# TensorE's program walked through once before it is run: a loop of two rounds over four parts

## The chip, the cores and the metric

The kernel runs on one core of one Trainium2 chip. The core has five engines with a program each: TensorE (PE in the profile, its weight loads PEld), VectorE (DVE), ScalarE (ACT), GpSimd (POOL) and SyncE (SP, which here only issues DMAs), and 16 DMA engines that move data between HBM and the core's memory. The metric is the device time of one execution in microseconds (us): 344.06 for the kernel before, the median of three runs (343.95 to 344.22).

## The reference

Two branches over the same two vectors x (2 x 1 x 512), mixed by a gate. Branch A is one decode step of attention with 32 heads over a cache of 4096 keys and values of length 128 for each of two batches; branch B is a small feed-forward network.

```python
g = _sigmoid((x * gate_w).sum(-1, keepdims=True))
q = (x @ wq).reshape(B, Sq, 32, 128).transpose(0, 2, 1, 3)
scores = jnp.einsum("bhqd,bhkd->bhqk", q, k_cache) * (128 ** -0.5)
o = jnp.einsum("bhqk,bhkd->bhqd", softmax(scores), v_cache)
a = o.transpose(0, 2, 1, 3).reshape(B, Sq, 4096) @ wo
b = jnp.einsum("bsf,fd->bsd", jnp.maximum(jnp.einsum("bsd,df->bsf", x, w1), 0), w2)
return g * a + (1 - g) * b
```

The caches are 64 MB each in bfloat16 and are read once; with the weights 145.4 MB go through the core.

## The kernel before

Each engine's program is collected first, as a list of operations in the order in which the functions at the end of the kernel are called (lines 703 to 740): gate, q_proj, ffn_h and ffn_relu, 64 k_turn, k_scores, softmax, v_unit(0), v_loop, gathers, the last two v_unit, project, last_rows, store. Then `resolve` numbers the signals and `emit` (line 88) writes the list of one engine after the other, with the waits for other engines' semaphores. `seen` keeps the highest value already waited for, so that no wait is written twice.

SyncE issues all large transfers in one list (lines 325 to 342): wq, w1, ten pieces of the key cache, nine of the value cache, then w2x (24 rows of 4 KB, in two transfers), wo in two parts, and w2 in three. A piece of 8 MB fills two of five regions of the buffer `kv`, a piece of 4 MB one; each is issued when TensorE has done with what the region held. For the third key piece that is the end of turn 3 of the scores (`pe_sc_3`).

VectorE transposes each key piece in 64 turns (line 471) into the four buffers of `kt`. TensorE multiplies them with the queries in a hardware loop of 8 rounds of 8 turns (k_scores, lines 481 to 511), the values with the probabilities in a hardware loop of 3 rounds of two pieces (v_loop, lines 587 to 608). `_Loop` holds the steps of such a loop, and `emit` opens it at line 98. Everything else of TensorE's program is written out: gate (4 transposes and a sum), q_proj and ffn_h (lines 402 to 455), one value piece before v_loop and two half pieces after it (v_unit, line 570), the gathers (line 639), project (line 664) and last_rows (line 683), whose last matmuls wait for the last piece of w2. GpSimd writes masked queries for every four turns (line 395), after ScalarE's copies (line 379).

The gate waits for x and gate_w; q_proj waits for wq and for the gate's `xTw`; the first transpose of a key piece stands behind the feed-forward network's first half in VectorE's list.

## Time and profile before

| what | value |
|---|---|
| median of three runs | 344.06 us |
| profiled execution | 344.31 us |
| its span, first to last instruction | 343.0 us |
| matmuls busy | 220.4 us |
| VectorE busy | 197.2 us |
| DMA, read from HBM | 145.43 MB, 424 GB/s over the span |
| mean granted TensorE clock | 0.846 |

The page of a profile gives busy times of the engines, the span in 40 slices, the DMA queues, the chain of work that ended last, groups of instructions and DMA issues. A group line holds the source line, engine, operation, what is written from what, a count, busy time and mean, then the idle time of the engine just before such instructions and what ended it. A line of a window holds the stretch, its length, the busy time of PE, PEld, DVE, ACT and POOL with their instructions, the granted clock, the DMA share and GB/s. A line of the timeline holds the start, the time to the end, and the instructions merged in it. Queue q1 carries SyncE's transfers; the queues of the kind "instruction" carry program text.

### The profile page before, as it was taken

The page shows a single profiled execution, that of the slowest core. Times are in us where ns is not written, and L with a number is a line of the kernel's source. Part 1 is how long each engine was busy: PE and PEld are TensorE (multiplying, and loading weights), DVE is VectorE, ACT ScalarE, POOL GpSimd, SP SyncE. Part 2 cuts the span into 40 slices and gives each one's busy share as a digit, 9 for nine tenths or more (in the row PEclk, how much of TensorE's full clock was granted, in tenths as well). Part 3 has the DMA queues.
Part 4 walks back from the last instruction along what each step waited for, and adds up shares of the span by engine and source line. Part 5 has one row for each costly group of instructions (what it writes and reads, how often), then busy time and mean ns, then how long its engine had stood idle before and what let it go on. Part 6 is the DMA issues. An engine that isn't in the chain of part 4 may idle for free.

```text
span 343.0 us, 2384 instructions
## 1 busy us (share of the span) xinstructions
PE 220.4 (64%) x1236; PEld 52.7 (15%) x764; DVE 197.2 (57%) x140; ACT 10.2 (3%) x30; POOL 13.9 (4%) x38
## 2 busy tenths in 40 slices
PE   0454629889969799799799463709073542809655
PEld 0110101111111111111111121102020110202312
DVE  0247249899889899698999496230606041110621
ACT  1060000000000000000000120000000000000000
POOL 6000000000000000000000200000000000000000
PEclk9986958999989999989899966967858595876968
DMA  8998989899999999898999999898989999999995
GB/s 314 451 495 367 489 367 489 374 481 436 420 466 390 429 428 481 374 489 371 485 420 436 451 405 468 382 481 374 481 382 481 420 436 451 405 420 432 412 418 213
DMA packets 3789, 145.50 MB, mean 424 GB/s; under 512 B 427, under 2 KB 560, under 8 KB 840
## 3 DMA queue, kind: packets, MB, share of 16 engines
q1 hardware_dynamic: 3778, 145.43, 98.4%
q8 instruction: 4, 0.07, 0.1%
q14 instruction: 1, 0.01, 0.0%
q10 hardware_dynamic: 6, 0.00, 0.0%
HBM read 145.43 MB, written 0.00 MB: 424 GB/s over the span
## 4 chain that ended last, share of the span: by engine, by line
DMA 59%; DVE 19%; PE 17%; issue 4%; ACT 0%; SPq 0%; DVEq 0%
DMA kv<-in_A_v_cache_dram 25%; DMA kv<-in_A_k_cache_dram 24%; DVE kt L471 16%; PE PS L477 7%; DMA kv<-in_B_w_dram 6%; PE PS L603 4%; DMA kv<-in_A_wq_dram 4%; PE PS L498 2%; PE PS L582 2%; PE PS L400 1%; DVE qrow L424 1%; DVE mpad L514 1%; ACT kt L526 0%; PE PS L484 0%; DVE kt L530 0%
## 5 line engine op out<-in xcount | busy, mean ns | idle before, releaser
L471 DVE STREAM_TRANSPOSE kt<-kv 128x2048 f32<-128x2048 f32 x64 | 141.2, 2274 | 24.5 <-DMA kv<-in_A_k_cache_dram 24.5
L498 PE MATMUL PS<-kt,qbuf 128*128 128x512 bf16 x256 | 107.0, 418 | 32.0 <-issue 27.2
L477 PE MATMUL PS<-kt,qbuf 128*128 128x512 bf16 x256 | 106.9, 418 | 0.0
L603 PE MATMUL PS<-kv,kt 128*64 128x512 bf16 x192 | 46.5, 462 | 56.7 <-DMA kv<-in_A_v_cache_dram 56.7
L615 DVE TENSOR_TENSOR kt<-PS,maskc 32x512 f32<-32x512 f32 (+1 forms) x21 | 14.5, 689 | 89.8 <-PE PS L477 82.2
L498 PEld LDWEIGHTS PS<-kt,qbuf 128*128 128x128 bf16 x256 | 25.9, 101 | 141.5 <-issue 141.5
L477 PE MATMUL PS<-kv,kt 128*64 128x512 bf16 x192 | 45.9, 456 | 0.0
L603 PEld LDWEIGHTS PS<-kv,kt 128*64 128x64 bf16 x192 | 14.9, 132 | 96.4 <-issue 96.4
L582 PE MATMUL PS<-kv,kt 128*32 128x512 bf16 x128 | 11.5, 522 | 10.3 <-DVE kt L543 7.3
L555 DVE TENSOR_TENSOR kt<-kt,mask 128x2048 bf16<-128x2048 bf16 (+1 forms) x10 | 16.1, 1654 | 0.0
L395 POOL TENSOR_TENSOR qbuf<-qs,mask 128x64 bf16<-128x64 bf16 x16 | 6.5, 406 | 162.2 <-PE PS L477 145.6
L627 DVE TENSOR_REDUCE kt<-kt 128x128 f32<-128x512 f32 x9 | 9.2, 1019 | 0.3
L526 ACT ACTIVATE kt<-PS,negm 128x512 bf16<-128x512 f32 x4 | 2.7, 685 | 172.8 <-DVE negm L522 172.8
L400 PE MATMUL PS<-kv,xTw 128*32 128x512 bf16 (+1 forms) x32 | 5.3, 693 | 3.5 <-DMA kv<-in_A_wq_dram 3.5
L582 PEld LDWEIGHTS PS<-kv,kt 128*32 128x32 bf16 x128 | 4.7, 125 | 16.3 <-DVE kt L543 7.8
L424 DVE CAST qrow<-PS 128x256 bf16<-128x256 f32 x2 | 2.6, 1508 | 5.7 <-PE PS L477 5.7
L643 PE MATMUL PS<-kt,selx 128*32 128x128 f32 x18 | 2.9, 293 | 4.0 <-DVE kt L627 3.0
L347 PE MATMUL PS<-ident,x_sb 3*128 3x3 bf16 x4 | 0.3, 167 | 8.2 <-DMA x_sb<-in_gate_w_dram 8.2
L350 DVE COPY xT<-PS 128x12 bf16<-128x12 bf16 x1 | 0.2, 171 | 8.5 <-PE PS L347 8.5
L700 ACT ACTIVATE out_sb<-PS 2x128 bf16<-2x128 f32 x2 | 0.5, 270 | 142.3 <-PE PS L679 142.2
L514 DVE TENSOR_REDUCE mpad<-PS 128x2 f32<-128x2048 f32 x1 | 2.3, 2291 | 3.1 <-PE PS L510 3.1
L477 PE MATMUL PS<-kv,xTw 128*32 128x512 bf16 (+1 forms) x24 | 3.7, 512 | 0.0
(78 smaller groups left out, 45.2 us busy)
## 6 DMA issues: line engine op xcount, KB each, us to landing
kv<-in_A_k_cache_dram SPq DMA_DIRECT2D x4, 4096.0 KB, 29.4
kv<-in_A_v_cache_dram SPq DMA_DIRECT2D x2, 4096.0 KB, 24.4
kv<-in_A_wq_dram SPq DMA_DIRECT2D x1, 4096.0 KB, 12.5
kv<-in_A_wo_dram SPq DMA_DIRECT2D x1, 3072.0 KB, 34.2
kv<-in_B_w_dram SPq DMA_DIRECT2D x1, 1376.0 KB, 15.3
kv<-in_A_wo_dram SPq DMA_DIRECT2D x1, 1024.0 KB, 36.2
kv<-in_B_w_dram SPq DMA_DIRECT2D x1, 896.0 KB, 21.4
kv<-in_B_w_dram SPq DMA_DIRECT2D x1, 256.0 KB, 21.7
```

The costliest lines, as they stand in the source:

```text
L395: pool(lambda g: g.tensor_tensor(out=out, in0=src, in1=mask, op=ALU.mult).then_inc(sem_q[k % 2], 1), waits=waits)
L400: return e.matmul(out, lhsT=xTw[:, t, :], rhs=rhs, start=(t == 0), stop=(t == 3), tile_position=(0, 32 * c))
L424: dve(lambda v, dst=dst, src=src: v.tensor_copy(out=dst, in_=src), waits=[f"pe_qr{half}"], signal=f"qrow{half}{e2}")
L471: dve(lambda v: v.transpose(out=dst, in_=pairs[:, h, 64 * a:64 * a + 64, :]).then_inc(sem_kt[i % SPAN], 1), waits=([f"pe_sc_{i - NKT}"] if ...
L477: return e.add_instruction(mybir.InstMatmult(start_tensor_calc=start, stop_tensor_calc=stop, tile_size=size, tile_position=at, ldweights=F ...
L498: ins = e.matmul(out, lhsT=lhsT, rhs=rhs, start=False, stop=False)
L514: dve(lambda v: v.tensor_reduce(out=mpad[:, 0:2], in_=psf(0, 128, 0, 4 * BANK).rearrange("p (par n) -> p par n", par=2), axis=AX.X, op=ALU ...
L555: ins = v.tensor_tensor(out=out, in0=src.unsqueeze(2).to_broadcast(shape), in1=mask8[:].unsqueeze(1).unsqueeze(3).to_broadcast(shape), op= ...
L582: ins = e.matmul(psf(32 * t, 32 * t + 32, V_BS[n] * BANK, 512), lhsT=v_weights(n)[:, j], rhs=rows[:, :, j, :], start=(j < 4), stop=(j >= n ...
L603: ins = e.matmul(out, lhsT=lhsT, rhs=rows[:, :, k, :], start=start, stop=stop, tile_position=(0, 64 * t))
L615: dve(lambda e: e.tensor_tensor(out=parts[p0:p1], in0=psf(p0, p1, bank * BANK, 512).rearrange("p (c d) -> p c d", c=4), in1=maskc[p0:p1].u ...
L627: dve(lambda e: e.tensor_reduce(out=X2[:, b, k, :], in_=parts.rearrange("p c d -> p d c"), axis=AX.X, op=ALU.add), waits=[f"dve_m{n}"], si ...
```

## The change

Only TensorE's program is written in another way. Three calls of `part()` mark places in its list of operations: after k_scores, after the first gather (with VectorE's `pr_clear`), and after the last v_unit. That makes four parts: the front with the scores; the first value piece, v_loop and the first gather; the last two half pieces of values; the projection and the last rows. `emit_twice` opens a loop of two rounds on TensorE alone. A register `walk` is 0 in the first round and 1 in the second. At the head of each part a comparison jumps to the part if `walk` is 1 and over it if not; a part ends with a jump to the place behind it. So in the first round no operation of the kernel is carried out, and in the second all are, in the old order with the old waits. The two hardware loops now lie within the new one. The other four engines' programs stay as they were.

```diff
-    def emit(self, engine, eng):
-        seen = {}
+    def emit_twice(self, engine, eng, parts):
+        ops, seen = self.ops[engine], {}
+        walk = self.nc.alloc_registers("walk", engines=(eng.engine,))
+        self.nc.regs_mov(walk, 0)
+        with self.nc.Fori(0, 2, engines=(eng.engine,)):
+            for a, b in zip([0] + parts, parts + [len(ops)]):
+                do, skip = f"{engine}_do_{a}", f"{engine}_skip_{a}"
+                self.nc.br_eq(walk, 1, on_true=do, on_false=skip, engines=(eng.engine,))
+                with self.nc.body(do, valid_engines=(eng.engine,)):
+                    self.emit(engine, eng, ops[a:b], seen)
+                    self.nc.br(skip, engines=(eng.engine,))
+                self.nc.switch_bb(skip)
+            self.nc.regs_mov(walk, 1)
+
+    def emit(self, engine, eng, ops=None, seen=None):
+        seen = {} if seen is None else seen
...
-        for op in self.ops[engine]:
+        for op in self.ops[engine] if ops is None else ops:
...
+    parts = []
+
+    def part():
+        parts.append(len(P.ops["pe"]))
+
...
     k_scores()
+    part()
...
     pr_clear()
+    part()
     v_unit(last - 1)
...
     v_extract(last)
+    part()
     project(range(-4, 0))
...
-        P.emit(name, eng)
+        if name == "pe":
+            P.emit_twice(name, eng, parts)
+        else:
+            P.emit(name, eng)
```

## The prediction

> **What bounds the kernel now.** I read the page's DMA parts first, because the DMA row of part 2 has no slice below 8 in 40 but one.

> ```profile
> span 343.0 us, 2384 instructions
> PE 220.4 (64%) x1236; PEld 52.7 (15%) x764; DVE 197.2 (57%) x140; ACT 10.2 (3%) x30; POOL 13.9 (4%) x38
> ...
> DMA  8998989899999999898999999898989999999995
> ...
> q1 hardware_dynamic: 3778, 145.43, 98.4%
> q8 instruction: 4, 0.07, 0.1%
> q14 instruction: 1, 0.01, 0.0%
> ```

> The reader is to see that the 16 DMA engines carry data for 98.4% of the span while TensorE works for 64% of it, and that four packets of program text, 0.07/4 MB or 16 KB each, travel on the same engines. Then I read the end, in stretches of half a microsecond, and the end of the chain.

> ```profile
> 338.00:338.50 0.50, 0.50 (x36) 0.38 (x28) 0.32 (x1) 0.00 (x0) 0.00 (x0) 1.00 0.75 283
> 338.50:339.00 0.50, 0.14 (x12) 0.07 (x8) 0.37 (x1) 0.00 (x0) 0.00 (x0) 1.00 0.51 203
> 339.00:339.50 0.50, 0.33 (x8) 0.03 (x8) 0.00 (x0) 0.00 (x0) 0.00 (x0) 1.00 0.37 139
> 339.50:340.00 0.50, 0.03 (x4) 0.04 (x8) 0.00 (x0) 0.00 (x0) 0.00 (x0) 1.00 0.40 119
> 340.00:340.50 0.50, 0.50 (x28) 0.34 (x28) 0.00 (x0) 0.00 (x0) 0.00 (x0) 1.00 0.11 37
> ...
> 319.32 21.59 DMA kv<-in_B_w_dram
> 340.92 0.04 issue
> 340.96 0.26 PE PS L679 x4
> ```

> The last two columns of the stretches are the DMA share and GB/s. The share fades over 2.3 us: the 16 engines do not end together, and the last of them releases the last matmuls. So the end is set by the **slowest single engine**, and the question is which engines a fetch of program text holds up.

> The trace's record of DMA packets (start, length, bytes, queue) answers that. A packet starts 3 to 4 ns before the one ahead of it on its engine ends, so the packets can be strung into 16 rows. Every row carries the same data but for the two w2x transfers, which lie on three rows alone. The rows end at 338.21, 338.25, 338.26, 338.30, 338.39, 338.40, 338.49, 338.62, 338.79, then 339.19, 339.36, 339.56, 339.81, and 340.07, 340.32, 340.49. The first nine end 334.5 us after they began their second packet (3.65 to 4.46 us). The late seven are explained one by one: 339.36 to 339.81 are the w2x rows (8 packets of 0.159 us more, 1.27 us); 339.19 is the row that the q14 fetch stopped at 119.5 us; and three different rows were stopped by q8: idle from 24.68 to 25.71, 209.61 to 210.68 and 323.13 to 324.13, with the next packet 0.47, 0.46 and 0.55 us longer than its kind. One fetch therefore costs its row 1.49, 1.53 or 1.55 us. The row that ends last (second packet at 4.46) would have ended at 338.96 and did so at 340.49 because of the first fetch. The fourth fetch, at 339.94, hit a row that was done.

> **The program and its fetches.** Counted once per loop, TensorE's program has about 126 instructions up to the score loop, 108 in it, 382 at the value loop's start, 580 at its end, 966 in all. From where its queue stood at each fetch I estimate that the fetches are asked for near 160, 415, 670 and 925, some 256 apart: each is asked for when the program enters a new block of that length, one block ahead, since no wait of TensorE ends with one.

> **The change, part by part.**
> Branches first.

> ```profile
> L98 PEldq COMPARE_BRANCH  x13: 76/208/309, 20.4 to 315.3; - x13
> L98 PEldq ALU_OP  x11: 36/36/42, 56.3 to 315.2; - x11
> L98 PEldq MOVE  x2: 29/31/33, 20.3 to 204.5; - x2
> ```

> Round one is two MOVEs, five or six branches of at most 0.31 us and one ALU_OP: under 2 us without fetches. Round two adds four compares and four jumps, at most 8 x 0.31 = 2.5 us if nothing hid them. They are hidden: the branch at 315.34 was taken by the sequencer while matmuls queued before it ran until 318.4, and the last of the new ones, ahead of the projection at about 331, falls into TensorE's wait for VectorE up to 333.3. I take 0.

> The jumps of round one land near 247, 606, 752 and 985. The first lies in a block that is there, the next three in blocks that are not. [...]

> ```profile
> 8.19 0.26 PE L347 MATMUL PS<-ident,x_sb 3*128 3x3 bf16 x4 [8.19 <-DMA x_sb<-in_gate_w_dram]
> 13.31 0.62 PE L400 MATMUL PS<-kv,xTw 128*32 128x512 bf16 x4 [3.54 <-DMA kv<-in_A_wq_dram]
> 30.25 0.59 PE L498 MATMUL PS<-kt,qbuf 128*128 128x512 bf16 x1 [5.78 <-issue]
> 27.84 8.89 DVE L471 STREAM_TRANSPOSE kt<-kv 128x2048 f32<-128x2048 f32 x4 [3.63 <-DMA kv<-in_A_k_cache_dram]
> 47.27 6.70 DVE L471 STREAM_TRANSPOSE kt<-kv 128x2048 f32<-128x2048 f32 x3 [10.54 <-DMA kv<-in_A_k_cache_dram]
> ```

> From the gate (8.19) to the query projection TensorE and VectorE need 1.6 us, and from there to VectorE's last work before the first transpose 10.9 us (13.31 to 24.2). A gate at T lets the transposes begin at T + 12.5, so T up to 15.3 changes nothing. Later than that, the scores of turn 3, at whose end (39.3) SyncE issues the next 8 MB, slip with it; but the piece before lands only at 47.27 and a transfer starts about 1 us after its issue, so another 6 us are covered. Queued behind this wait are SyncE's whole list and nothing else. I take 0, bounds 0 and 4 us (T = 25).

> What is left is the engines' rows. Before, three fetches fall into the data stream. After, it depends on whether the blocks walked over stay:

> - If they stay, round one fetches four blocks early and round two none. Four rows stopped once instead of three: 340.3 to 340.5 as before, sum 0.
> - If they don't, round one fetches four, the return two (the first block and the next), round two three more before the stream ends: nine in place of three. The three rows hit so far are among the four whose second packet began latest (4.04, 4.28, 4.29, 4.46), so I estimate that the fetches go round four rows: two or three each. Two stops end at 338.79 + 2 x 1.53 = 341.9, three on the latest row, the first of them partly ahead of its data, at 342.0 to 343.5. Against 340.49 that is +1.4 to +3.0, and I take +1.8, nearer to two stops than to three.

> Does a trace show which? The value loop is 198 instructions long and by the estimates above holds a border between two blocks; its second and third rounds fetched nothing. So at least two, and by my reading three, blocks stay; for the six blocks of a return to the front there is no row.

> [...]

> The profiled execution took 344.31 us around its span of 343.05, 0.25 over the median of 344.06. Its sum is 344.31 + 1.8 = 346.1; against the median 345.8.

> **The rivals.**
> *The blocks stay* (no change): 344.1, from 343.8 to 344.5. For it: the loop's quiet rounds. Against: it needs twice the reach that those show.
> *The fetches get ahead of the data* (faster): no row has data before 1.83 us, and a stop then costs nothing. Without stops by q8 the last row is the w2x row at 339.81: 340.49 - 339.81 = 0.68 less, 343.4; with a fetch less to slow the tail a little lower. It decides if at most one of the early fetches costs a row that starts late. [...]
> [...]
> *A w2x row is hit*: 339.81 + 1.53 = 341.3, +0.9, 344.9; it needs fetches that wander over all 16 rows.

> **How the numbers follow.** Refetching (with the w2x case) 0.50; blocks stay 0.27; ahead of the data 0.16; late TensorE 0.07. About 0.2%, 0.7 us, is what a measurement here tells from no change. Refetching and lateness are slower but for 0.02; blocks staying is the same but for 0.02 slower; ahead of the data is faster by its place at the limit, two thirds over. Summed, with a little for unknown gains: faster 0.15, same 0.28, slower 0.57. Refetching's own range is 344.9 to 347.1; the 8 in 10 range takes in the two below it, to 0.2 under 343.4, and leaves out only the upper half of the late case, from 347.6.

> **What would show it.** Right: q8 counts nine or ten packets instead of four, several within the first 20 us and again near 205 and 320; rows that end near 342; the last matmuls (the line of the last rows) start at 342 or later; the first score matmul stays at 30.3. Blocks stay: five q8 packets or fewer, all ahead of 20 us, and last matmuls at 340.8 to 341.0. Ahead of the data: the same count with the share of DMA falling to nothing before 340. [...] It would be wrong if a jump costs far more than a fetch's own time, or if fetches go to rows other than the late four.

## The result

The changed kernel takes 345.95 us in the median of 18 runs, the kernel before 344.07 in 18: a ratio of 1.0054, with a 95% interval of 1.0045 to 1.0064. Its single times spread more, from 344.09 to 347.42 against 343.93 to 344.37. The profiled execution took 345.74 around a span of 344.5 us, 1.43 over that of before.

The page of the changed kernel, where the prediction looked first: the span, the DMA row, and the queues with their packets, MB and share.

```profile
span 344.5 us, 2400 instructions
...
DMA  8999989999898999989999999989899998989995
...
q1 hardware_dynamic: 3778, 145.43, 98.1%
q8 instruction: 4, 0.07, 0.1%
```

The reader is to see that q8 still moves four packets, as many as before: the refetching that the forecast took for the likeliest case did not happen. The record of DMA packets has the four at 5.29, 11.29, 17.93 and 24.08 us, where before they lay at 24.67, 209.61, 323.12 and 339.94. Which block a packet brings is not in the record.

What the fetches do to TensorE's sequencer stands in the line of the new comparisons (minimum, median and longest duration in ns, first and last start), and what follows in the timeline of the changed kernel (start, length, what, and the idle time before it) and in SyncE's waits (sum, times, longest; the kernel before first).

```profile
L95 PEldq COMPARE_BRANCH  x8: 63/216/6658, 1.1 to 329.3; - x8
```

```profile
21.17 0.26 PE L361 MATMUL PS<-ident,x_sb 3*128 3x3 bf16 x4 [21.17 <-issue]
36.30 0.40 PE L512 MATMUL PS<-kt,qbuf 128*128 128x512 bf16 x1 [1.67 <-issue]
33.90 8.88 DVE L485 STREAM_TRANSPOSE kt<-kv 128x2048 f32<-128x2048 f32 x4
46.88 13.28 DVE L485 STREAM_TRANSPOSE kt<-kv 128x2048 f32<-128x2048 f32 x6 [4.10 <-DMA kv<-in_A_k_cache_dram]
```

```profile
SPq L329 <- PE PS L477: 268.0, 14, 37.0
```

```profile
SPq L343 <- PE PS L491: 268.9, 14, 42.3
```

Of the four jumps of the first round, three wait 6.14, 5.95 and 6.66 us (the trace's records of that line), with one of the first three packets of q8 in each wait; the first takes 0.36. The gate starts at 21.17 us instead of 8.19. It drags the first transposes from 27.84 to 33.90 and the scores of turn 3 after them, and SyncE's longest wait, the one ahead of the third key piece, ends at 45.00 instead of 39.72 (42.3 us long instead of 37.0). By then 12 of the 16 DMA rows have run out of data: the packet record has them end between 44.40 and 44.84 and start again between 45.96 and 46.85. In the kernel before, no row stands still there. The windows from 40 to 50 us give the DMA share and GB/s in their last two columns, the first line of the kernel before, the second of the changed one. They are a coarse sign: a window counts a packet in full where it starts, so a share can pass 1, and the split kernels below show 0.87 and 0.88 in this window with no row dry. By the packet record the rows were busy for 1.00 of it before and for 0.88 now.

```profile
40.00:50.00 10.00, 0.32 (x1) 0.10 (x1) 2.73 (x2) 0.00 (x0) 0.11 (x1) 0.72 1.03 446
```

```profile
40.00:50.00 10.00, 5.38 (x21) 1.03 (x10) 5.90 (x4) 0.00 (x0) 0.33 (x1) 0.91 0.87 347
```

The loss stays to the end: by the packet record the first 20 MB are in 2.21 us later than in the kernel before, 60 MB 1.99 and 145 MB 1.77. The tail keeps its form:

```profile
339.50:340.00 0.50, 0.50 (x32) 0.50 (x24) 0.40 (x1) 0.00 (x0) 0.00 (x0) 0.50 0.99 389
340.00:340.50 0.50, 0.50 (x20) 0.22 (x15) 0.29 (x1) 0.00 (x0) 0.00 (x0) 0.50 0.85 311
340.50:341.00 0.50, 0.46 (x8) 0.00 (x0) 0.00 (x0) 0.00 (x0) 0.00 (x0) 0.50 0.39 145
341.00:341.50 0.50, 0.08 (x8) 0.08 (x12) 0.00 (x0) 0.00 (x0) 0.00 (x0) 0.50 0.24 90
341.50:342.00 0.50, 0.50 (x28) 0.43 (x26) 0.00 (x0) 0.00 (x0) 0.00 (x0) 0.75 0.11 39
342.00:342.50 0.50, 0.46 (x23) 0.19 (x12) 0.00 (x0) 0.00 (x0) 0.00 (x0) 1.00 0.00 0
```

The last data packet ends at 341.89 instead of 340.49, 1.40 later, and the span is 1.43 longer.

### The profile page after: what moved, and what is told of

The parts are those of the page before. It is cut to its first block, busy times and chain, and to the rows that moved or that the text cites. A ratio compares the mean times of both kernels' runs of the same rounds, so it can differ in the third digit from the quotient of the medians.

```text
span 344.5 us, 2400 instructions
## 1 busy us (share of the span) xinstructions
PE 218.8 (64%) x1236; PEld 52.9 (15%) x764; DVE 197.1 (57%) x140; ACT 10.2 (3%) x30; POOL 13.9 (4%) x38
## 3 DMA queue, kind: packets, MB, share of 16 engines
q1 hardware_dynamic: 3778, 145.43, 98.1%
HBM read 145.43 MB, written 0.00 MB: 422 GB/s over the span
## 4 chain that ended last, share of the span: by engine, by line
DMA 56%; DVE 22%; PE 15%; issue 6%; ACT 0%; ACTq 0%; DVEq 0%
DMA kv<-in_A_v_cache_dram 25%; DMA kv<-in_A_k_cache_dram 23%; DVE kt L485 19%; DMA kv<-in_B_w_dram 6%; PE PS L491 5%; PE PS L617 4%; DMA x_sb<-in_gate_w_dram 2%; PE PS L596 2%; PE PS L414 1%; PE PS L512 1%; DVE qrow L438 1%; DVE mpad L528 1%; ACT kt L540 0%; DVE kt L544 0%; DVE kt L557 0%
## 5 line engine op out<-in xcount | busy, mean ns | idle before, releaser
L617 PE MATMUL PS<-kv,kt 128*64 128x512 bf16 x192 | 45.5, 453 | 58.2 <-DMA kv<-in_A_v_cache_dram 58.2
L491 PE MATMUL PS<-kv,kt 128*64 128x512 bf16 x192 | 44.8, 445 | 0.0
L414 PE MATMUL PS<-kv,xTw 128*32 128x512 bf16 (+1 forms) x32 | 5.3, 690 | 0.0
L684 PE MATMUL PS<-kv,oW 128*2 128x512 bf16 x24 | 2.7, 625 | 1.7 <-DMA kv<-in_A_wo_dram 1.7
```

The lines of the kernel that those rows point to most:

```text
L414: return e.matmul(out, lhsT=xTw[:, t, :], rhs=rhs, start=(t == 0), stop=(t == 3), tile_position=(0, 32 * c))
L491: return e.add_instruction(mybir.InstMatmult(start_tensor_calc=start, stop_tensor_calc=stop, tile_size=size, tile_position=at, ldweights=F ...
L617: ins = e.matmul(out, lhsT=lhsT, rhs=rows[:, :, k, :], start=start, stop=stop, tile_position=(0, 64 * t))
```

## The experiments

The trace left a theory, called L below: the walk costs time only because TensorE starts late, so that SyncE issues the third key piece after the rows have run dry. Its rivals: F, the early stops of the rows by the fetches cost it; B, the added branches and nested loops do.

**Late without a walk.** The kernel before, with GpSimd kept busy ahead of the gate:

```diff
     pool(lambda g: g.memset(selx[:], 0.0), signal="c_selx")
+    idle = sb("idle", [128, 1280], dt.bfloat16)
+    for n, size in enumerate([1280, 1280, 1280, 1280, 1280, 1280, 1280, 1280, 1280, 1280, 1280, 1280, 1280]):
+        pool(lambda g, size=size: g.memset(idle[:, 0:size], 0.0), waits=[f"c_idle{n - 1}"] if n else [], signal=f"c_idle{n}")
...
-               waits=(["c_i16"] if t == 0 else []), dwaits=([(sem["x"], 16), (sem["gw"], 16)] if t == 0 else []),
+               waits=(["c_idle12"] if t == 0 else []), dwaits=([(sem["x"], 16), (sem["gw"], 16)] if t == 0 else []),
```

> The kernel before, with no walk; GpSimd fills an unused tile 13 times and TensorE's gate waits for the last fill, so that it starts near 21 us as it does in the changed kernel. Theory L (the walk costs time only because TensorE starts late, so that SyncE issues the third key piece late and the DMA rows run dry near 45 us): gate at 21 us, issue of the third key piece near 45 us instead of 39.7, 345.5 to 346.5 us. Rival F (the early fetches' stops on the DMA rows cost it): 344.1. Rival B (the added branches and the nesting of the loops cost it): 344.1.

Measured: 347.98 us against 343.89, ratio 1.012 (1.0103 to 1.0137), above the range expected by L. The gate came later than meant, at 22.74, and the third key piece at 46.56. The windows from 40 to 50 us:

```profile
40.00:50.00 10.00, 6.78 (x27) 1.35 (x14) 7.39 (x4) 0.00 (x0) 0.33 (x1) 1.00 0.57 216
```

No branch and no early fetch is in this kernel (its q8 packets lie at 35.2, 212.9, 325.3 and 343.0 us), and it loses more than the changed kernel does. Lateness alone is enough. Three more lengths of the same delay, 9, 11 and 16 fills, give the shape:

> The kernel before, no walk, with 9 fills of GpSimd ahead of the gate instead of 13 (gate 22.7 us there): gate near 18 us. Theory L: turn 3 ends at the gate plus 23.8 us, 41.7, and the first data of the third piece come 1 us later, before the rows run dry at 44.5: 343.8 to 344.2 us. If any delay of the front cost its own length: about 2 us more than before.

> The kernel before with 11 fills ahead of the gate: gate near 20.3 us, turn 3 ends near 44.1. Theory L: first data of the third piece at 45.1, 0.5 us after the rows run dry; the rows that are late anyway lose nothing, so 344.1 to 345.0 us. If the cost set in with any delay in proportion: about 3 us over before.

> The same with 16 fills: gate near 26.4 us, turn 3 ends near 50.2. Theory L: rows dry from 44.5 to about 51.5, and 3.6 us more than with 13 fills (4.1 over before): 351.5 us. If other covers take it up later: below 349.

| fills | gate, us | third key piece issued | rows dry, mean of the 16, us | first packets longer, mean of the 16, us | over the kernel before, us |
|---|---|---|---|---|---|
| (before) | 8.19 | 39.72 | 0 | 0 | 0 |
| 9 | 17.88 | 41.83 | 0 | 0 | 0.07 (1.0000, 0.9991 to 1.0009) |
| 11 | 20.30 | 44.29 | 0.72 | 0.53 | 1.45 (1.0040, 1.0025 to 1.0055) |
| (the change) | 21.17 | 45.00 | 1.22 | 0.48 | 1.88 (1.0054, 1.0045 to 1.0064) |
| 13 | 22.74 | 46.56 | 2.92 | 0.66 | 4.09 (1.0120, 1.0103 to 1.0137) |
| 16 | 26.41 | 50.27 | 6.58 | 0.72 | 7.80 (1.0227, 1.0208 to 1.0245) |

The fourth and fifth columns are from the packet record: how long the rows stood with nothing to carry, and by how much the first 64 KB packet of each dry row was longer than the 2.42 us of a running row.

The window of the longest delay:

```profile
40.00:50.00 10.00, 7.94 (x32) 1.54 (x16) 10.00 (x5) 0.00 (x0) 0.00 (x0) 1.00 0.30 126
```

A gate 9.7 us late is free, and from 13 to 16 fills each microsecond of later issue costs about one: 3.71 us of issue, 3.71 of time, with 0.6 us of uncertainty on each of the two times. Between lies the edge. With 11 fills I had expected at most 0.9 and got 1.45: 15 rows ran out between 44.42 and 45.01 and took up again between 45.25 and 46.11, but the packets that started a row anew took longer (2.6 to 3.5 us on eleven of the twelve rows in the changed kernel, 2.42 on a running row), which I had left out. The two columns together account for all but 0.2 to 0.5 us of each time. The changed kernel fits into the row of times by its issue at 45.00: between 11 and 13 fills a straight line would give it 2.3, and it costs 1.9, a difference that lies within the intervals.

**The walk without the lateness.** Two edits give SyncE more data to issue ahead of turn 3, each in both kernels. The first moves half a key piece forward:

```diff
-    k_pieces = [(0, lo, "Bh"), (1, both, "A"), (2, both, "B"), (0, hi, "C"), (3, both, "A"), ...
+    k_pieces = [(0, lo, "Bh"), (1, both, "A"), (0, hi, "C"), (2, both, "B"), (3, both, "A"), ...
```

> The changed kernel with SyncE's 4 MB half of the first key piece (region C, which waits for the query projection alone) ahead of the third key piece: 9.7 us more of data are queued when the third piece is issued. Theory L: gate still near 21 us, but no stretch without DMA near 45 us, 343.9 to 344.5 us. Rivals F and B: 345.5 to 346.5 as before.

> The same order of pieces in the kernel before, as the control for it. All theories: 343.8 to 344.4 us, since its rows never run dry.

Measured: 348.31 with the walk, 348.51 without, against 343.89: both 4.4 to 4.6 us slower, and both missed what was expected. The new order moves a dry stretch to 93 us, in both kernels alike. The windows from 90 to 100 us, the kernel before first, then its reordered version, then the reordered version with the walk:

```profile
90.00:100.00 10.00, 6.86 (x27) 1.31 (x13) 7.37 (x4) 0.00 (x0) 0.46 (x1) 0.95 0.98 426
```

```profile
90.00:100.00 10.00, 7.79 (x29) 1.43 (x14) 8.31 (x5) 0.00 (x0) 0.33 (x1) 0.89 0.56 216
```

```profile
90.00:100.00 10.00, 8.34 (x36) 1.65 (x17) 8.31 (x5) 0.00 (x0) 0.34 (x1) 1.00 0.56 210
```

With the walk the gate is as late as ever (21.33) and no row runs dry near 45 us. But the pair doesn't settle it, since a dry stretch at 93 us can swallow what the walk cost ahead of it. So the second edit leaves the order alone and issues the third key piece in two halves, the first of which waits for the feed-forward network's first half only (the landing count of that region is raised by one to match):

```diff
     for kind, n, u, halves, region in pieces:
+        if (kind, n) == ("k", 2):
+            for half, part, wait in ((0, "B", "pe_h"), (1, "Bh", f"pe_sc_{turn_end[0]}")):
+                sp(lambda e, half=half, part=part: e.dma_start(piece_sb((half,), part), piece_in("k", 2, (half,))).then_inc(landed["k", 2][0], 16),
+                   waits=[marker(wait)])
+            continue
```

> The changed kernel with the third key piece issued as two transfers of 4 MB: the first waits for the feed-forward network's first half alone, the second for the scores of turn 3 as the whole piece did. Order and amount of data are unchanged; 9.7 us more are queued when turn 3 ends. Theory L (the walk costs time only through the rows that run dry near 45 us): gate still near 21 us, turn 3 still ends near 45 us, no dry stretch anywhere, 343.7 to 344.4 us. Rival F (stops of the four early fetches on the rows): 345 to 346.

> The same split in the kernel before, as the control. All theories: 343.8 to 344.2 us, no dry stretch before or after the edit.

Measured: 344.13 with the walk and 344.23 without, against 344.10: ratios of 1.0002 (0.9993 to 1.0011) and 1.0003 (0.9994 to 1.0012). With the walk the gate starts at 21.29 and the half that waits for turn 3 is issued at 45.13, as late as in the changed kernel, but the other half has been queued since 32.99, and no row runs dry in either kernel. SyncE's waits ahead of the two halves, with the walk:

```profile
SPq L344 <- PE PS L419: 30.2, 1, 30.2
SPq L344 <- PE PS L496: 11.8, 1, 11.8
```

So the jumps, the four early fetches and the branches of the second round cost nothing that these runs can tell from zero, once the rows have data; L stands, and F and B fall. The version with both edits is as fast as the kernel before and not faster. Its profiled execution, at 345.32, was slower than its ten other runs (343.94 to 344.82); some rows have packets of 2.5 to 4.1 us at 209 us there, and I can't say why.

**One part instead of four.** All three marks are left out, so that the first round is one jump over the whole program:

```diff
     k_scores()
-    part()
...
     pr_clear()
-    part()
...
     v_extract(last)
-    part()
```

> The changed kernel with one part instead of four: the first round makes one jump over the whole program. Theory L: one wait of about 6 us in place of three, gate between 9 and 15 us (the later if the return has to wait too), third key piece issued by 40 us, 343.9 to 344.5 us. Rival F: as many early fetches or more (the blocks jumped over have to come later), 344.5 to 346. Rival B: a quarter of the branches, 344.5.

Measured: 344.02 against 343.89, ratio 1.0003 (0.9993 to 1.0012). The jump waits 5.30 us and the gate starts at 8.05, when x has landed. The line of the comparisons, and q8 on its page:

```profile
L95 PEldq COMPARE_BRANCH  x2: 75/2686/5297, 1.1 to 7.0; - x2
```

```profile
q8 instruction: 6, 0.10, 0.1%
```

One wait hides under the landing of x, three do not. The six fetches are two early ones (3.96 and 9.87 us) and then four near the places where the kernel before has them (27.8, 209.3, 322.0, 339.5). By this count, jumping over blocks did not bring them in here, and the two early fetches saved no later one; after the change's walk from block to block there were no later ones.

**An attempt at the late rows.** If rows stopped by a fetch set the end, taking data off the last rows should move it. The last two pieces of w2 were issued as 24 and 104 partitions each (the transfers take partitions p0 to p1, and the last matmuls wait for both):

```diff
-    for name, r0, r1 in (("w2b", 0, 7), ("w2c", 7, 9), ("w2d", 9, 10)):
+    for name, r0, r1, p0, p1 in (("w2b", 0, 7, 0, 128), ("w2c", 7, 9, 0, 24), ("w2c", 7, 9, 24, 128),
+                                 ("w2d", 9, 10, 0, 24), ("w2d", 9, 10, 24, 128)):
...
```

> The kernel before with the last two pieces of w2 issued as 24 and 104 partitions each instead of 128. If a transfer over 24 partitions lies on the first 12 rows and one over 104 on the first 13, the last rows carry eight packets less of 0.085 and of 0.046 us each (1.05 us), the first 12 rows 0.26 us more. Row theory of the prediction (the end is set by the rows that a fetch of program text stopped, 1.5 us each, and these are late rows of the 16): the last row ends at 340.1 instead of 340.5 us, 343.7 us against 344.1. If the end is not set by those rows: 344.1 or, by the w2x rows, up to 344.4.

Measured: 345.14 against 344.23, ratio 1.0027 (1.0016 to 1.0037), the other way. The small packets now run beside those of the larger piece ahead of them: its 7 KB packets take 0.39 to 0.59 us in the last 3 us instead of 0.27 to 0.29, and five rows end between 340.88 and 341.05. That says nothing on whether stopped rows set the end, since more than the distribution changed; it stays an account of the ends in one profile.

## Why the prediction was right or wrong

The time was forecast at 345.8 and came at 345.95, but by another mechanism than the one that was priced; the number is right by luck.

- *What bounds the kernel* held: the DMA rows set the end, and the loss is a stretch in which they had nothing to carry.
- *Branches at 0* held: with the rows fed, the walking kernel took 344.13 against 344.10.
- *The blocks don't stay, nine fetches for three, +1.8* is the step that failed. There were four fetches, none after 24.08 us. The return jump to the front took 0.225 us, so the front was still there. The fourth packet came 3.75 us after the third wait's end and ended no wait; which block it brought the trace doesn't show. After it the second round ran through the whole program without a fetch by q8. So in this run the blocks, six by the estimate, stayed. The rival of staying blocks had this right, and its 0 is what the split showed for the walk itself.
- *A late TensorE at 0, bounds 0 and 4 us (T = 25),* was the other miss. The T of that bound rests on an estimate of mine of what a jump waits, which no run shows. The runs showed waits of 6.14, 5.95 and 6.66 us, a round one that ends at 20.9 and a gate at 21.17; and a straight line between the gates of 13 and 16 fills (22.74 and 26.41) gives 6.4 us for a gate at 25, an estimate. From the packet record, the fetch starts 3.6 to 4.3 us after the jump (two or three full packets of its row run in between) and takes 0.93 to 0.96, and TensorE goes on only 1.36 to 1.47 us after its packet's end. No run splits the 3.6 to 4.3 us into the asking for a block and the wait for the row.
- *A gate at T moves the transposes to T + 12.5* held: 21.17 + 12.5 = 33.7, measured 33.90.
- *T up to 15.3 changes nothing, and another 6 us are covered* was too wide. I read the moment at which the rows run dry from the landing of the second key piece (47.27), which only its last row sets, a row that a fetch had stopped. The other rows run dry at 44.40 to 44.84. The runs put the edge between 41.83 and 44.29 us of issue, a gate between 17.9 and 20.3; 44.40 less the 0.96 from the issue to the first row's data gives 43.4, an estimate that lies between.
- Long waits and a short cover together made TensorE late, which the forecast gave 0.07: the first transposes moved from 27.84 to 33.90, and the first score matmul to 36.30, which the forecast said would stay at 30.3. The last matmuls at 342.38 are as late as refetching would have had them, for the other reason.
- The single times' spread stays open. The three waits could vary from one execution to the next, but the gates of the three profiles with the four-part walk lie at 21.17, 21.29 and 21.33, and no second profile of the changed kernel itself was taken.
- The list of the rows whose second packet began latest leaves out one at 4.16, later than the 4.04 in it. It served the estimate that the fetches go round four rows, which no run tested.

## What to carry to other kernels

The cover of a delay in this kernel was not the time until the next transfer had landed (47.27 us) but until the first DMA row had run out (44.40), less the time from issue to first data (0.96); read it from the rows before calling a delay of the front free. A delay beyond that cover cost about its own length (3.71 us of time for 3.71 of issue, from 13 to 16 fills), in a kernel whose DMA rows carried data for 98.4% of the span, though the delayed engine worked for only 64% of it. To tell a delay's cost from that of the code that makes it, delay the engine without the code, and feed the rows with the code in place.
